# A front written in another order, and weight conversions, batch 0's tail and local scores at other steps, in an attention and mixer kernel

## The chip, the core and the metric

The kernel runs on one core of a Trainium2 chip. The metric is the device time of one execution in microseconds. The core has a matrix engine (PE, with PEld for its weight loads), a vector engine (DVE), a scalar engine (ACT), a third elementwise engine (POOL), and queues that start transfers (SP, and ACT's own). Each engine works through its own instructions in order; an instruction that waits holds all that stand behind it on that engine.

## What is computed

Attention of 8 batches with 8 heads over 576 positions of 64 numbers, and behind it a mixer block on the 576 x 512 result of each batch:

```python
scores = scale * np.matmul(q, k.transpose(0, 1, 3, 2))
rel = pos[:, None] - pos[None, :]
mask_local = (rel >= 0) & (rel < stride)                       # heads 0 to 3, stride 32
mask_strided = (rel >= 0) & (pos[None, :] % stride == pos[:, None] % stride)   # heads 4 to 7
attn = softmax(np.where(masks, scores, -1e9))                  # softmax stands for the written-out lines
x = (attn @ v).transpose(0, 2, 1, 3).reshape(B, S, H * D)
xt = x.transpose(0, 2, 1)
h = np.maximum(xt @ w_tok1, 0.0) @ w_tok2                      # token mix, 576 -> 256 -> 576
u = x + h.transpose(0, 2, 1)
out = u + np.maximum(u @ w_ch1, 0.0) @ w_ch2                   # channel mix, 512 -> 1536 -> 512
```

The mixer's weights come as 64-bit floats, everything else as 32-bit ones.

## The kernel before, in words

**Products.** A wide matrix product is made of three passes in a reduced float format: each operand is split into a high part and a low part, and high x high, high x low and low x high are added (names end in `h` and `l`, as `w1h`, `w1l`).

**Weights.** They must be converted from 64 bits and split first. `convert` does it for a piece of at most 128 x 512 in three stages: the load (L118); on ACT the low byte (L128) and the high word (L131), on DVE the sign byte (L129); then the putting together on DVE (L133), the cast to the high part on ACT (L142) and the subtraction that leaves the low part on POOL (L143). `pieces` lists the 22 pieces that are still to be converted when the channel mix of batch 0 begins: nine of `w1`, twelve of `w2`, and the tail of the second token weight. `do_pieces(i)` runs stage two of piece i+1, stage three of piece i, and the loads of pieces three or four further on.

**The front** (to about 44 us) loads batch 0's operands, computes its attention (`s0`, `s1` strided heads, `l0`, `l1` local heads), converts the token weights and the first three pieces of `w1` (`e0` to `e7`), does the token mix (`L` for the local half, `S` for the strided half, `m0` to `m3`), and begins the pieces (`p0` to `p3`). Each of these is a generator, and the text `order` says which one takes its next step; `b` is a product without use that keeps PE busy, and `x` reloads the strided half of the attention's result from DRAM. All engines' queues and SP's are filled in this order.

**The channel mix.** `mlp` runs 24 blocks for each batch: `up_proj(fc)` (12 products, `w1`, L825) and `down_proj(fc)` (12 products, `w2`, L837), as up 0, up 1, up 2, down 0, up 3, down 1, and so on. Behind an up block ACT makes `gh` (L828) and DVE `gl` (L829); the single bank of `up_proj` (`h`) is free for the next up block when both are done. After block n the work that stands under step n in `after` is put into the queues, in its middle that of step n - 0.5. Step n has nothing to do with time: it is a place in each engine's order. In batch 0 this work is:

- the conversions, `do_pieces(i)`, by a formula in i;
- batch 0's tail, `tok2_tail` (L632 on PE, L633 on ACT, L634 on DVE, and a store of SP, L635), the last 64 positions;
- batch 1's strided heads (`lanes`): scores (L391, L394, L400, L401, L404), transposition (L410, copies L412), values (L421, L428 to L432, stores L442);
- batch 1's remaining local heads (`rest`, four units): load, scores (L197, then L216 on DVE and L219 on ACT), transposition (L224, copy L226), values (L232, L237 to L247, store L258);
- from step 12 the load of batch 1's rows (L546, L549), from 15 its token mix (`tok1`: splits L561 on ACT, L564 and L567 on DVE, products L579 on PE, then L587 and L588; `tok2`: L613, L618 at steps 20 and 22);
- from step 14 the later batches' strided heads on POOL and DVE (products L453, sums L506 and L533; loads L467 in ACT's queue).

Score, transposition and value products take their banks (`t`) from three in turn. From the channel mix on, SP's order is made by a scheduler from the program; that of PE, DVE, ACT and POOL is the written one.

## Time and profile before

| | us |
|---|---|
| median of three runs (795.97 to 799.19) | 797.36 |
| the profiled execution | 799.21 |
| its span in the trace | 797.4 |
| PE busy | 770.7 |
| DVE, ACT, POOL busy | 463.4, 241.4, 379.4 |

The span is the time from the first to the last instruction in the trace; what lies around it is 1.8 us. A busy PE isn't PE at its peak: its clock has two levels, and the granted clock of a stretch is given as a share of the higher one. A timeline row shows when an instruction (or a run of like ones) began, how long it took, and in brackets how long its engine stood idle before it and what ended that.

### The profile page before, as it was taken

The page shows a single profiled execution, that of the slowest core. Times are in us where ns is not written, and L with a number is a line of the kernel's source. Part 1 is how long each engine was busy: PE and PEld are TensorE (multiplying, and loading weights), DVE is VectorE, ACT ScalarE, POOL GpSimd, SP SyncE. Part 2 cuts the span into 40 slices and gives each one's busy share as a digit, 9 for nine tenths or more (in the row PEclk, how much of TensorE's full clock was granted, in tenths as well). Part 3 has the DMA queues.
Part 4 walks back from the last instruction along what each step waited for, and adds up shares of the span by engine and source line. Part 5 has one row for each costly group of instructions (what it writes and reads, how often), then busy time and mean ns, then how long its engine had stood idle before and what let it go on. Part 6 is the DMA issues. An engine that isn't in the chain of part 4 may idle for free.

```text
span 797.4 us, 14592 instructions
## 1 busy us (share of the span) xinstructions
PE 770.7 (97%) x5916; PEld 623.6 (78%) x5916; DVE 463.4 (58%) x963; ACT 241.4 (30%) x496; POOL 379.4 (48%) x287
## 2 busy tenths in 40 slices
PE   7889997999999999999999999999999999999998
PEld 4767776877778888887888888788888888888886
DVE  4756658778588776876687758776652233113112
ACT  4776864132112322331223122332232222102010
POOL 2232357958877883778478766667500000202000
PEclk9999999999999999999999999999999999999999
DMA  9776682235802471356215521645043211101001
GB/s 323 239 253 212 189 256 81 94 108 152 247 22 97 117 232 43 111 148 241 83 67 162 146 83 54 191 157 152 0 127 105 55 47 72 53 1 53 1 1 53
DMA packets 72731, 96.20 MB, mean 121 GB/s; under 512 B 33560, under 2 KB 47704, under 8 KB 72664
## 3 DMA queue, kind: packets, MB, share of 16 engines
q1 hardware_dynamic: 72088, 93.38, 37.7%
q10 hardware_dynamic: 576, 1.90, 0.6%
q8 instruction: 46, 0.75, 0.4%
q14 instruction: 21, 0.17, 0.1%
HBM read 67.79 MB, written 27.46 MB: 119 GB/s over the span
## 4 chain that ended last, share of the span: by engine, by line
PE 76%; DVE 9%; DMA 5%; POOL 4%; issue 2%; ACT 2%; SPq 1%; DVEq 0%; ACTq 0%; POOLq 0%
PE acc L837 31%; PE h L825 28%; PE t L618 5%; PE t L579 5%; POOL sprod L453 4%; PE t L825 2%; DMA w_raw<-in_wt 2%; DMA sa<-in_qs 1%; PE t L357 1%; DVE sa L533 1%; DVE xhl L567 1%; PE t L632 1%; DVE w_f L133 1%; DVE w_rest L129 1%; DVE ss L506 1%
## 5 line engine op out<-in xcount | busy, mean ns | idle before, releaser
L453 POOL TENSOR_TENSOR sprod<-sa,ss 128x576 f32<-128x576 f32 (+8 forms) x108 | 153.5, 1460 | 84.9 <-issue 49.0
L453 POOL TENSOR_TENSOR sprod<-sa 128x576 f32<-128x576 f32 (+8 forms) x108 | 160.8, 1520 | 38.4 <-DVE ss L506 13.5
L837 PE MATMUL acc<-gh,w2h 128*128 128x512 f32 x432 | 170.8, 395 | 0.0
L829 DVE SCALAR_TENSOR_TENSOR gl<-h,gh 128x512 fp32r<-128x512 f32 x99 | 68.1, 688 | 176.3 <-ACT gh L828 176.0
L837 PE MATMUL acc<-gl,w2h 128*128 128x512 f32 x432 | 168.5, 390 | 0.0
L837 PE MATMUL acc<-gh,w2l 128*128 128x512 f32 x432 | 168.4, 390 | 0.0
L825 PE MATMUL h<-uh,w1h 128*128 128x512 f32 x396 | 157.8, 399 | 2.5 <-DVE gl L829 2.4
L825 PE MATMUL h<-ul,w1h 128*128 128x512 f32 x396 | 155.0, 391 | 0.0
L825 PE MATMUL h<-uh,w1l 128*128 128x512 f32 x396 | 154.6, 390 | 0.0
L828 ACT ACTIVATE gh<-h 128x512 fp32r<-128x512 f32 x99 | 59.1, 597 | 289.0 <-PE h L825 289.0
L837 PEld LDWEIGHTS acc<-gh,w2h 128*128 128x128 f32 x432 | 81.3, 188 | 17.3
L837 PEld LDWEIGHTS acc<-gh,w2l 128*128 128x128 f32 x432 | 81.2, 188 | 17.2
L506 DVE TENSOR_REDUCE ss<-sprod 128x9 f32<-128x576 f32 (+8 forms) x108 | 80.2, 777 | 24.5 <-POOL sprod L453 24.4
L837 PEld LDWEIGHTS acc<-gl,w2h 128*128 128x128 f32 x432 | 81.3, 188 | 16.5 <-DVE gl L829 0.2
L825 PEld LDWEIGHTS h<-uh,w1h 128*128 128x128 f32 x396 | 74.5, 188 | 20.7 <-DVE gl L829 4.6
L533 DVE TENSOR_REDUCE sa<-sprod 128x64 f32<-128x576 f32 (+8 forms) x108 | 80.1, 777 | 17.2 <-POOL sprod L453 16.9
L825 PEld LDWEIGHTS h<-ul,w1h 128*128 128x128 f32 x396 | 74.5, 188 | 16.0
L825 PEld LDWEIGHTS h<-uh,w1l 128*128 128x128 f32 x396 | 74.5, 188 | 14.6
L646 POOL TENSOR_TENSOR x<-x,xhl 128x512 f32<-128x512 f32 x4 | 5.0, 1284 | 115.1 <-DMA x<-u 115.1
L579 PE MATMUL t<-xhl,t1h 128*128 128x512 f32 (+1 forms) x134 | 41.2, 390 | 5.1 <-DVE xhl L564 2.5
L561 ACT CAST xhl<-x 128x512 fp32r<-128x512 f32 (+1 forms) x37 | 21.9, 609 | 42.7 <-PE t L579 36.4
L567 DVE TENSOR_TENSOR xhl<-x,xhl 128x512 fp32r<-128x512 f32 (+1 forms) x30 | 29.3, 996 | 9.2 <-ACT xhl L561 9.2
(190 smaller groups left out, 872.3 us busy)
## 6 DMA issues: line engine op xcount, KB each, us to landing
out_t<-ot SPq DMA_DIRECT2D x35, 256.0 KB
w_raw<-in_w SPq DMA_DIRECT2D x17, 512.0 KB
lqk<-in_qkU SPq DMA_DIRECT2D x9, 832.0 KB
x<-x SPq DMA_DIRECT2D x28, 256.0 KB
lv<-in_vU SPq DMA_DIRECT2D x9, 780.0 KB
xhl<-in_w SPq DMA_DIRECT2D x7, 512.0 KB
x<-lv SPq DMA_DIRECT2D x36, 96.0 KB
xtl<-lv SPq DMA_DIRECT2D x36, 96.0 KB
```

The source lines that it names most:

```text
L129: nc.vector.tensor_scalar(out=y_b[:, :, 3], in0=raw_b[:, :n, 7], scalar1=128, scalar2=None, op0=ALU.bitwise_and)
L453: i = nc.gpsimd.tensor_tensor(op=op, **operands)
L506: nc.vector.tensor_reduce(out=s_t[:, i, :i + 1], in_=pr.rearrange("p (n d) -> p n d", d=D), axis=AX.X, op=ALU.add)
L533: nc.vector.tensor_reduce(out=o_t[:, i], in_=pr.rearrange("p (d n) -> p d n", n=i + 1), axis=AX.X, op=ALU.add)
L561: nc.scalar.copy(out=xh, in_=x)
L567: apart.append(nc.vector.tensor_tensor(out=xlo, in0=x, in1=xh.bitcast(F32), op=ALU.subtract))
L579: nc.tensor.matmul(ph[m], l[:, c, P * m:P * m + P], r, start=(c == 0 and k == 0), stop=(c == NSC - 1 and k == len(terms) - 1))
L618: nc.tensor.matmul(pu, l[:, cs], r[:, m, :MAIN], start=(turned and m == 0 and k == 0), stop=(m == 1 and k == 2), skip_group_check=True)
L825: nc.tensor.matmul(ph, l[:, cc, fs], r, start=(cc == 0 and k == 0), stop=(cc == NCC - 1 and k == 2))
L828: nc.scalar.activation(out=gh, in_=ph, func=AF.Relu)
L829: nc.vector.scalar_tensor_tensor(out=gl, in0=ph, scalar=0.0, in1=gh.bitcast(F32), op0=ALU.max, op1=ALU.subtract)
L837: nc.tensor.matmul(acc[cc], l[:, fc, cs], r, start=(fc == 0 and k == 0), stop=(fc == NFC - 1 and k == 2))
```

## The change

Three tables are changed; no instruction of the computation is added or taken away but twelve more rows of keep-busy products and their weight loads on PE.

- `order`, the front, is written anew. The strided pair `s1` goes first, the operands of both local pairs are loaded ahead of the first token weight, the second token weight's conversion goes behind both local softmaxes, and the reload `x` and the later weights' loads move as well.
- `do_pieces(i)` stood at int(1.8 i)/2, so 0, 0.5, 1.5, 2.5, ... up to 18.5; it stands at int(1.6 + 1.48 i)/2, so 0.5, 1.5, 2, 3, 3.5, ... up to 16. The staging memory is given back at step 18, before at 20.
- Batch 0's tail moves from step 2 to 3. The scores of the four local units move from steps 1.5, 4.5, 7.5, 9.5 to 2.5, 5.5, 8.5, 10, their transpositions and values with them (the last one's values stay at 11.5), and the loads of units two to four from 2, 5, 7 to 3, 6, 9.

```diff
--- before.py
+++ after.py
@@ -769,9 +769,9 @@
                 nc.gpsimd.tensor_copy(out=masks[:, 64 * c:64 * c + 64], in_=mask_sb[:, FIRST.get(c, 0)])
 
         order = """
-            s0 s1 s1 l0 s0 s0 s1 e0 s0 l0 e0 l0 s0 l1 e1 s1 b e2 l0 e0 e1 l1 l1 b s1 e3 e2 e4 l1 b b e1 s0 s1 e2 e3 e5
-            l0 l1 e4 b b b b m0 L x L L L e3 L e4 L l0 m1 S m3 m0 e6 m0 S e5 S S S e7 e6 S m2 e5 m1 m2 e6 p0 m3 m1 l1 m2 m3 e7 e7
-            p1 p2 p3 p0"""
+            s1 s0 s1 s1 s0 s0 l0 s1 b l0 l0 b s1 b l1 e0 e1 s0 l0 e0 l1 l1 b e0 s0 b b b e2 e3 e1 e2 s1 s0
+            l1 e4 e1 e2 l0 b l1 b b b b b x e3 e5 m0 L e4 L L L e6 e3 e4 L m1 L m3 e7 S m0 l0 S m0
+            e5 S S p0 S e6 e5 m2 S m1 e7 e6 m2 m1 l1 m2 m3 m3 p0 e7 p1 p2 p3"""
 
         for i, k in enumerate(order.split()):
             if i == 3:
@@ -982,7 +982,7 @@
         def do_tail(cc):
             x_next["u"].append(tail_u(up0, ps_t, x_next["x"], cc))
 
-        at(2 if b == 0 else 0, tok2_tail, ps_t, x_t, h, b)
+        at(3 if b == 0 else 0, tok2_tail, ps_t, x_t, h, b)
         if b + 1 < B:
             at(12, load_next, b + 1)
             steps = (15, 16, 17, 18, 19, 19) if b < 2 else range(14, 20)
@@ -999,15 +999,15 @@
                 at(20 + cc, do_tail, cc)
         if b == 0:
             for i in range(len(pieces)):
-                at(int(1.8 * i) / 2, do_pieces, i)
+                at(int(1.6 + 1.48 * i) / 2, do_pieces, i)
             for i in (0, 1, 2, 3, 4, 6, 7, 8):
                 at(i, next, lanes[0], None)
-            for g, steps in zip(rest, ((0, 1.5, 2.5, 3.5), (2, 4.5, 5.5, 6.5), (5, 7.5, 8.5, 9.5), (7, 9.5, 10.5, 11.5)), strict=True):
+            for g, steps in zip(rest, ((0, 2.5, 3.5, 4.5), (3, 5.5, 6.5, 7.5), (6, 8.5, 9.5, 10.5), (9, 10, 11, 11.5)), strict=True):
                 for i in steps:
                     at(i, next, g, None)
             at(12, first_ends)
             at(14, first_strided)
-            at(int(0.9 * len(pieces)) + 1, staging_ends)
+            at(18, staging_ends)
         for k, steps in UNITS[b].items():
             for n, i in enumerate(steps):
                 if i is not None:
```

The first place is DVE's order at the front, from the first strided softmax on: L129 takes the sign bytes of a weight (`w_raw`), L283 and L284 are a local softmax, L428 to L432 divide a strided result. Before:

```order
L129 TENSOR_SCALAR w_rest0_101<-w_raw_223 128x512
L283 TENSOR_REDUCE lm_282<-pair_238 128x10
L284 TENSOR_TENSOR ls_281<-pair_238,lm_282 128x2x5x64
L428 TENSOR_SCALAR em_190<-pair_286 128x12
L430 RECIPROCAL em_190<-em_190 128x12
L432 TENSOR_TENSOR ex_311<-pair_286,em_190 128x3x128 x2
L133 SCALAR_TENSOR_TENSOR w_f_234<-w_f_234,w_rest0_101 128x512
L129 TENSOR_SCALAR w_rest1_102<-w_raw_319 128x512
L283 TENSOR_REDUCE lm_392<-pair_348 128x10
L284 TENSOR_TENSOR ls_391<-pair_348,lm_392 128x2x5x64
```

and after:

```order
L283 TENSOR_REDUCE lm_277<-pair_233 128x10
L284 TENSOR_TENSOR ls_276<-pair_233,lm_277 128x2x5x64
L428 TENSOR_SCALAR em_185<-pair_282 128x12
L430 RECIPROCAL em_185<-em_185 128x12
L432 TENSOR_TENSOR ex_307<-pair_282,em_185 128x3x128 x2
L129 TENSOR_SCALAR w_rest0_101<-w_raw_316 128x512
L283 TENSOR_REDUCE lm_384<-pair_340 128x10
L284 TENSOR_TENSOR ls_383<-pair_340,lm_384 128x2x5x64
L133 SCALAR_TENSOR_TENSOR w_f_335<-w_f_335,w_rest0_101 128x512
```

The first local softmax has no weight ahead of it any more, and the second one the first weight instead of the second.

The second place is PE's order in the channel mix of batch 0, from the middle of block 2 (`up_proj(2)`) on; L197 are the scores of the first local unit, L632 the tail, L410 the strided transposition. Before:

```order
L197 MATMUL t<-lqk 32x64 x16
L825 MATMUL h<-uh,w1h 128x512
L825 MATMUL h<-uh,w1l 128x512
L825 MATMUL h<-ul,w1h 128x512
L825 MATMUL h<-uh,w1h 128x512
L825 MATMUL h<-uh,w1l 128x512
L825 MATMUL h<-ul,w1h 128x512
L632 MATMUL t<-hh_142,t2h 128x512
L632 MATMUL t<-hl_143,t2h 128x512
L632 MATMUL t<-hh_144,t2h 128x512
L632 MATMUL t<-hl_145,t2h 128x512
L410 MATMUL t<-ident,es 128x128 x6
```

and after, where block 2 has ended and block 3 (`down_proj(0)`, L837) comes:

```order
L410 MATMUL t<-ident,es 128x128 x6
L837 MATMUL acc_816<-gh,w2h 128x512
L837 MATMUL acc_816<-gl,w2h 128x512
L837 MATMUL acc_816<-gh,w2l 128x512
L837 MATMUL acc_817<-gh,w2h 128x512
L837 MATMUL acc_817<-gl,w2h 128x512
L837 MATMUL acc_817<-gh,w2l 128x512
L197 MATMUL t<-lqk 32x64 x16
L837 MATMUL acc_818<-gh,w2h 128x512
```

The scores moved from the middle of block 2 into the middle of block 3, the tail behind that block, and the strided transposition is now the first thing behind block 2.

The third place is ACT's order from `gh` of block 14 on; L128, L131 and L142 are conversions, L467 the loads of the strided heads, L561 the splits of batch 1's rows. Before, `w_raw_1528`, `w_raw_1615` are the pieces 17 and 18:

```order
L828 ACTIVATE gh_1623<-h_1601 128x512
L128 ACTIVATE w_rest1_102<-w_raw_1528,small_69 128x512
L131 ACTIVATE w_f_1627<-w_raw_1528 128x512
L142 CAST w1h_72<-w_f_1608 128x4x128
L467 DMA sa_1637<-in_ks 128x1152
L467 DMA sa_1636<-in_qs 128x1152
L467 DMA sa_1638<-in_vs 128x1152
L561 CAST xhl_1659<-x_1565 128x512
L128 ACTIVATE w_rest0_101<-w_raw_1615,small_69 128x512
L131 ACTIVATE w_f_1662<-w_raw_1615 128x512
L142 CAST w2h_794<-w_f_1627 128x512
```

and after, where `w_raw_1614`, `w_raw_1631`, `w_raw_1657` are the pieces 19, 20 and 21:

```order
L828 ACTIVATE gh_1646<-h_1633 128x512
L128 ACTIVATE w_rest1_102<-w_raw_1614,small_69 128x512
L131 ACTIVATE w_f_1650<-w_raw_1614 128x512
L142 CAST w1h_72<-w_f_1624 128x4x128
L467 DMA sa_1660<-in_ks 128x1152
L467 DMA sa_1659<-in_qs 128x1152
L467 DMA sa_1661<-in_vs 128x1152
L128 ACTIVATE w_rest0_101<-w_raw_1631,small_69 128x512
L131 ACTIVATE w_f_1674<-w_raw_1631 128x512
L142 CAST w2h_799<-w_f_1650 128x512
L561 CAST xhl_1689<-x_1586 128x512
L128 ACTIVATE w_rest1_102<-w_raw_1657,small_69 128x512
```

Before the first split one piece is begun and one cast is done, now two of each. In SP's order the load of piece 17 stood between batch 1's last rows; now pieces 17 and 18 stand ahead of the last local store (L258) and pieces 19 to 21 behind all of the rows.

## Rows read from the trace of the kernel before

**Rows 1.** the page: span, and share of the engines

```profile
span 797.4 us, 14592 instructions
...
PE 770.7 (97%) x5916; PEld 623.6 (78%) x5916; DVE 463.4 (58%) x963; ACT 241.4 (30%) x496; POOL 379.4 (48%) x287
```

**Rows 2.** busy time by stretch: engine busy us (x instructions), granted clock, DMA share, GB/s

```profile
49.80:69.90 20.10, 17.68 (x208) 13.00 (x208) 11.34 (x36) 12.35 (x26) 5.06 (x6) 0.83 0.67 212
69.90:101.20 31.30, 30.04 (x396) 22.84 (x395) 20.67 (x71) 24.58 (x49) 13.56 (x11) 1.00 0.68 204
101.20:112.10 10.90, 10.90 (x49) 8.82 (x47) 4.40 (x8) 6.55 (x11) 4.86 (x4) 1.00 0.79 220
112.10:137.20 25.10, 19.16 (x85) 14.86 (x85) 19.40 (x21) 13.71 (x24) 17.75 (x13) 1.00 0.43 148
...
56.20:62.90 6.70, 5.95 (x17) 4.33 (x16) 2.90 (x14) 5.23 (x13) 0.46 (x1) 0.50 0.60 200
138.00:141.40 3.40, 3.40 (x10) 2.63 (x9) 1.96 (x3) 0.59 (x1) 3.40 (x3) 0.50 0.60 180
```

**Rows 3.** timeline of DVE at the front: start us, us, instruction [idle before <-releaser]

```profile
13.43 0.47 DVE L129 TENSOR_SCALAR w_rest<-w_raw 128x512 uint8<-128x512 uint8 x1 [3.12 <-DMA w_raw<-in_wt]
...
19.22 0.80 DVE L129 TENSOR_SCALAR w_rest<-w_raw 128x512 uint8<-128x512 uint8 x1 [1.76 <-DMA w_raw<-in_wt]
19.91 0.80 DVE L283 TENSOR_REDUCE lm<-pair 128x10 f32<-128x640 f32 x1
```

**Rows 4.** timeline of PE at the front

```profile
29.15 0.50 PE L579 MATMUL t<-eqk,t1h 128*128 128x256 f32 x2 [0.90 <-ACT eqk L561]
...
44.30 0.39 PE L825 MATMUL h<-uh,w1h 128*128 128x512 f32 x1
```

**Rows 5.** timeline of PE, steps 1.5 to 2 of batch 0

```profile
54.15 0.30 PE L197 MATMUL t<-lqk 64*32 64x64 f32 x2 [0.87 <-DVE gl L829]
55.24 0.45 PE L197 MATMUL t<-lqk 64*32 64x64 f32 x30 [0.80 <-DVE es L401]
...
58.91 0.80 PE L632 MATMUL t<-hh,t2h 128*128 128x512 f32 x1 [0.75 <-POOL t2h L143]
```

**Rows 6.** timeline of ACT: one conversion, and the copies behind a transposition

```profile
83.05 0.85 ACT L412 COPY es<-t 128x384 f32<-128x384 f32 x2
...
86.39 0.87 ACT L128 ACTIVATE w_rest<-w_raw,small 128x512 uint8<-128x512 uint8 x1
87.12 0.66 ACT L131 ACTIVATE w_f<-w_raw 128x512 f32<-128x512 f32 x1
88.19 0.62 ACT L142 CAST w2h<-w_f 128x512 fp32r<-128x512 f32 x1 [0.41 <-DVE w_f L133]
```

**Rows 7.** timeline of PE, step 9.5

```profile
92.99 0.45 PE L197 MATMUL t<-lqk 64*32 64x64 f32 x30 [1.26 <-DVE lx L247]
```

**Rows 8.** timelines of SP and ACT around step 14

```profile
100.86 0.36 SPq L258 DMA_DIRECT2D x<-lx  x1
...
104.58 0.36 SPq L118 DMA_DIRECT2D w_raw<-in_w  x1
...
110.46 0.90 ACT L128 ACTIVATE w_rest<-w_raw,small 128x512 uint8<-128x512 uint8 x1 [3.01 <-DMA w_raw<-in_w]
```

**Rows 9.** timeline of PE, steps 16 to 20

```profile
113.66 0.74 PE L579 MATMUL t<-xhl,t1h 128*128 128x512 f32 x2 [1.40 <-ACT xhl L561]
...
128.99 0.73 PE L579 MATMUL t<-xhl,t1h 128*128 128x512 f32 x2 [1.08 <-DVE xhl L564]
...
136.81 0.44 PE L613 MATMUL t<-ident,x 128*128 128x128 f32 x2 [3.45 <-DVE hl L588]
```

**Rows 10.** timelines of POOL and DVE, steps 18 to 20

```profile
122.78 1.57 POOL L453 TENSOR_TENSOR sprod<-sa 128x576 f32<-128x576 f32 x1
...
122.99 1.68 DVE L129 TENSOR_SCALAR w_rest<-w_raw 128x512 uint8<-128x512 uint8 x1
...
130.31 2.03 DVE L133 SCALAR_TENSOR_TENSOR w_f<-w_f,w_rest 128x512 uint32<-128x512 uint32 x1
```

## The prediction

> **What bounds the kernel now.** I read the page first: PE is busy 770.7 of 797.4 us [rows 1]; DVE, ACT and POOL are far below. So only stretches in which PE waits, or runs at half clock, can give time back, and the change touches only what comes before about 140 us (the front, and batch 0's 24 blocks). Second, the table by stretch [rows 2]. Blocks 0 and 1 of batch 0 end at 49.8; block 4 (`up_proj(3)`) at 69.9, block 12 at 101.2, block 16 at 112.1, and the next batch's token mix reaches its second half at 137.2. The first of these stretches runs at a mean clock of 0.83, with 56.2 to 62.9 at 0.50, the 1.2 GHz level; 138.0 to 141.4 is at 0.50 as well. From 112.1 to 137.2 PE is busy 19.16 of 25.1 us. Third, the timelines of PE name the waits. At the front the first mixing product starts at 29.15 and block 0 at 44.30 [rows 4]. In block 2 and behind it PE waits 0.87, 0.80 and 0.75 us [rows 5], and then the clock falls. At step 9.5 it waits 1.26 for a bank [rows 7]. At steps 16 to 20 it waits 1.40, 1.08 and 3.45 [rows 9], the last two for DVE, whose conversions run at 1.5 to 2.0 us each there [rows 10].
>
> **The change, part by part.** All sums are against the profiled execution (799.21 us: a span of 797.4 and 1.8 around it); the median of the runs is 797.36, 1.85 less, and I carry the difference over to it.
>
> *Front order: -3.0 us.* Before, DVE's queue holds the second local softmax (L283) behind the high bytes of the second token weight, which land at 19.2 [rows 3]. After, only the first token weight stands ahead of it, and it is loaded behind the local operands. It is then the tenth load of the queue with 4.73 MB up to its end; before, 3.38 MB landed at 13.4 and 5.25 MB at 19.2 [rows 3], so it lands at about 17.6 and L283 starts some 1.9 us earlier than its 19.91. The two local value products no longer stand back to back on PE, so DVE divides the first while PE makes the second: about 0.9 more, which brings the first mixing product [rows 4] to about 26.3. Four transpositions move ahead of the last mixing products, 0.2. Downstream the conversions of the token and first up weights keep their place relative to PE, so nothing takes this back before block 0. Bounds: -1.2 (the weight lands as late as 19.2 and only the overlap counts) to -3.5. The added keep-busy products lie in gaps.
>
> *Local scores at 2.5 and batch 0's tail at 3: -4.9 us.* Both leave the place where their banks and the tail weight are not ready. Gone are the three waits, 2.4 us [rows 5], and the half clock that follows them: 6.7 us with PE busy 5.95 [rows 2] is 3.0 us lost. New: the first down block now follows block 2 directly, and its third product needs the low part of `w2` chunk 0, which POOL makes after ACT's cast; I put that at 0.7 us, and a bank for the local scores at 0.3. -5.4 + 1.0 is -4.4; laid out by durations, the stretch of 20.1 us shrinks to 14.8, -5.3; I take the middle. Bounds: -1 (the waits reform at the new place and the clock falls again) to -5.5.
>
> *Conversions at 0.74 step apiece: +3.5 us in steps 4 to 12.* One conversion is 1.8 us of ACT (starts 86.39, 87.12, 88.19 less a wait of 0.41, and 0.53 for the cast) [rows 6], plus that wait where the multiply-out on DVE is late. Before, ACT is busy 12.35 + 24.58 + 6.55 = 43.5 of the 62.3 us to 112.1 [rows 2]. After, four more conversions fall into the same steps: 7.2 us, and 21 waits of 0.41 are 8.6, together 59 of 62. ACT, off the path so far, becomes nearly full, and it does two conversions, 3.6 us, where before there was one between an exponential and the copies that free its banks. That is where I expect new PE waits: step 7 (transpositions behind a late exponential) 0.6, step 7.5 (local value products, whose bank is freed by L412, half of 0.85 [rows 6]) 2.2, step 8.5 a bank behind DVE 0.85, step 10 the last local operands, whose load now stands in SP's queue behind six strided stores and a weight, 0.8; and 0.3 elsewhere. The 1.26 of step 9.5 [rows 7] goes. Sum 4.75 - 1.26 = +3.5. Bounds: 0 (ACT keeps up) to +8 (each up block also waits for its `gh`).
>
> *Steps 12 to 16:* PE ran without a gap, 10.9 of 10.9 [rows 2], and should again: nothing.
>
> *Steps 14 to 20: -2.3 us.* Before, ACT stands 3.01 us at 110.46 for a weight that SP issued at 104.58, in the midst of the next batch's rows, which wait for the store of 100.86 [rows 8]: 5.9 us from issue to use. After, one weight more goes ahead of that store, and the next (the third last) goes behind the rows. I expect the same wait on ACT, from the same store, and behind it not one conversion but two before the first split of the next batch (L561): 1.8 + 0.4 more. So the 1.40 becomes about 3.65: +2.25. Behind it, though, no conversion is left for steps 18 to 20: the last cast comes at step 16 instead of 18.5, ahead of most of POOL's strided products. DVE's splits and `hl` are then on time, and 1.08 + 3.45 [rows 9] go. Sum -2.3. Bounds: -4.5 to +3 (the wait grows and the 3.45 stays).
>
> *Clock: 0.* The half clock of 138.0 to 141.4 cost 3.4 / 2 = 1.7 us [rows 2] and came behind 3.45 us of waiting. It goes with it, but a wait of 3.65 at step 16 should bring one of the same price. Bounds: -1.7 to +2.
>
> Later batches keep their order on every engine; the shift passes to the end one to one. Sum: -3.0 - 4.9 + 3.5 - 2.3 + 0 = **-6.7**: 792.5 for a profiled execution, **790.7** as a median.
>
> **A rule against the change.** Rows: DVE's L129 starts at 122.99 inside a POOL product that runs 122.78 to 124.35, and takes 1.68 us; L133 took 2.03 at 130.31 [rows 10], against 0.47 for L129 at 13.43 [rows 3]. So where POOL is at work, a conversion's steps on DVE can be held. The Trainium skill ("SBUF — State Buffer", SBUF: two separate sides) says that DVE in a two-port mode or with two SBUF inputs and GpSimd lock a shared port pair against each other for a whole instruction; by that rule denser conversions, each with a POOL subtraction, would hold each other, and the trace agrees at the rows named.
>
> **The rivals.**
>
> 1. *ACT keeps up.* The waits of steps 7 to 10 don't form (+3.5 becomes 0): 787.2. For it: ACT had idle time next to its waits; against it: 59 of 62 us. Chance 0.15.
>
> 2. *The end of batch 0 keeps its waits.* `hl` (L588) still stands on DVE behind three sums of POOL's strided products; if the first of these start late, the 3.45 and the 1.08 remain: -6.7 + 4.5, 795.2. For it: POOL's strided work begins only after all conversions; against it: its loads are issued in the same step. Chance 0.28.
>
> 3. *Slower: DVE and POOL hold each other.* Each of the 17 conversions of steps 3 to 16 takes 1.0 us more (1.5 to 2.0 in place of 0.5 to 0.7) and ACT waits for it: 59 + 17 = 76 us where there were 62.3, +13.5 in place of -4.9 + 3.5; with -3.0 and -2.3 that is about +8: 805. It decides from about ten of the 17 (3 us of slack, then the 6.7). Against it: in 44 to 112 us few of DVE's conversion steps are stretched, since POOL starts only after ACT's cast, when DVE is past its own. Chance 0.10.
>
> 4. *The new numbers move less than they say* (an engine's order stays as it was): the order shown above excludes it for DVE, PE and ACT. Chance 0.02.
>
> **How the numbers follow.** The forecast, 790.7, has 0.45. Its own bounds (front -1.2 to -3.5, tail -1 to -5.5, conversions 0 to +8, end -4.5 to +3, clock -1.7 to +2) seldom fall together: about 785 to 797. To hold 8 in 10 the range takes in rivals 1 and 2 and leaves out rival 3: **785.0 to 798.5**. Half a per cent, 4.0 us, is about what a measurement of this kernel tells from no change, so faster means below 793.4: most of the forecast (0.39), rival 1 (0.15) and a little of rival 2: 0.57. Within: 0.32. Slower, above 801.3: rival 3 and a remainder, 0.11.
>
> **What would show each step right or wrong.** Front: the first mixing product near 26.3 and block 0 near 41.3; wrong, if DVE's L283 of the second pair still starts after 19. Steps 1 to 4: a clock of 1.00 there and about 15 us from the end of block 1 to the end of block 4. Steps 4 to 12: a wait of about 2 us for L412 at the value products of step 7.5, and a stretch of about 35 us for 31.3. Step 16: a wait of 3 to 4 us for ACT's L561, half clock behind it. Step 20: no wait for L588. The forecast is wrong most easily by ACT's queue, which I laid out by hand, and by where the clock falls.

## The result and the profile after

The changed kernel takes 805.05 us (median of seven runs, 800.92 to 805.69) against 797.36: a ratio of 1.0084, 95% interval 1.0057 to 1.0111. It is slower by 0.8%, where 790.7 was forecast; the time lies above the whole range. Run again beside 23 runs of the kernel before (e5 below) it took 802.10, ratio 1.0055 (1.0035 to 1.0075). The profiled execution is 805.69 us with a span of 803.9, 6.5 more than before. Three executions of the runs below that lie far off the rest (two at a granted clock of 0.75 throughout, 951 us, one of them the profiled one of e9, and one of the kernel before at 3870 us) are left out of the ratios. The page after, against [rows 1]:

```profile
span 803.9 us, 14601 instructions
PE 775.7 (96%) x5915; PEld 627.1 (78%) x5921; DVE 462.6 (58%) x963; ACT 241.6 (30%) x496; POOL 378.8 (47%) x287
```

PE is 5 us busier for the same products of the computation (the new front adds five keep-busy products, each under 0.7 us), so clock is lost as well as time. The table by stretch, with the columns of [rows 2] (us, busy time of PE, PEld, DVE, ACT, POOL, granted clock, DMA share, GB/s): blocks 2 to 4, blocks 5 to 12, blocks 13 to 16, and from there to the second half of the next batch's token mix; behind the dots three pieces of these at about half clock:

```profile
50.94:65.70 14.76, 14.12 (x175) 10.88 (x175) 8.51 (x27) 10.08 (x22) 4.04 (x4) 1.00 0.66 194
65.70:107.60 41.90, 35.18 (x428) 25.12 (x427) 25.83 (x81) 28.93 (x58) 16.45 (x14) 0.92 0.64 197
107.60:119.00 11.40, 11.16 (x48) 8.56 (x46) 4.25 (x6) 5.04 (x8) 4.74 (x4) 1.00 0.65 195
119.00:144.90 25.90, 20.42 (x83) 16.73 (x84) 15.40 (x21) 11.89 (x20) 18.29 (x14) 0.87 0.46 164
...
84.50:88.00 3.50, 3.45 (x48) 2.31 (x52) 0.89 (x5) 0.62 (x2) 0.97 (x1) 0.59 0.78 213
98.30:103.00 4.70, 4.62 (x73) 3.29 (x74) 1.53 (x13) 2.95 (x8) 2.53 (x2) 0.64 0.53 177
122.00:130.00 8.00, 5.52 (x14) 4.38 (x15) 4.26 (x5) 5.93 (x10) 5.13 (x4) 0.57 0.69 276
```

Beside [rows 2], between the same places in the program (the windows above meet them within 0.2 us):

| | before | forecast | after | e5, the same again |
|---|---|---|---|---|
| block 0 starts | 44.3 | 41.3 | 45.2 | 45.1 |
| blocks 2 to 4 | 20.2 | 14.8 to 15.2 | 14.8 | 14.9 |
| blocks 5 to 12 | 31.3 | 34.8 | **41.9** | **39.3** |
| blocks 13 to 16 | 10.9 | 10.9 | 11.4 | 11.3 |
| block 16 to the tail products of batch 1 (L632) | 44.1 | 41.8 | 43.5 | 41.3 |
| L632 to the end | 641.3 | 641.3 | 641.6 | 641.8 |

Blocks 2 to 4 came out as laid out, the front gained nothing, and blocks 5 to 12 took three times the extra that was forecast. The waits that do it, in the timeline of PE, against [rows 5, 7, 9]:

```profile
57.54 0.50 PE L837 MATMUL acc<-gh,w2l 128*128 128x512 f32 x1 [0.64 <-POOL w2l L143]
...
67.97 0.56 PE L232 MATMUL t<-lv,ls 64*32 64x65 f32 x32 [0.72 <-ACT ls L226]
...
80.33 0.88 PE L410 MATMUL t<-ident,es 128*128 128x128 f32 x6 [1.58 <-ACT es L404]
...
84.55 0.46 PE L232 MATMUL t<-lv,ls 64*32 64x65 f32 x30 [1.72 <-ACT es L412]
...
91.16 0.45 PE L197 MATMUL t<-lqk 64*32 64x64 f32 x30 [0.37 <-DVE ex L432]
...
98.38 0.62 PE L197 MATMUL t<-lqk 64*32 64x64 f32 x32 [2.07 <-DMA lqk<-in_qkT]
...
124.48 1.22 PE L579 MATMUL t<-xhl,t1h 128*128 128x512 f32 x2 [5.50 <-ACT xhl L561]
```

The waits of [rows 5] and the 1.08 and 3.45 of [rows 9] are gone, the 1.40 is 5.50, and blocks 5 to 12 hold five waits of 0.37 us or more where they held one.

**How the wait of step 7 comes about.** ACT, in front of the exponential of the strided scores (L404), and DVE beside it:

```profile
73.55 0.88 ACT L128 ACTIVATE w_rest<-w_raw,small 128x512 uint8<-128x512 uint8 x1
...
75.34 1.09 ACT L219 ACTIVATE ls<-ls,lm 128x64 f32<-128x64 f32 x4
76.31 0.61 ACT L828 ACTIVATE gh<-h 128x512 fp32r<-128x512 f32 x1
79.53 0.75 ACT L404 ACTIVATE es<-es 128x648 f32<-128x648 f32 x1 [2.62 <-DVE es L401]
```

```profile
76.95 0.69 DVE L829 SCALAR_TENSOR_TENSOR gl<-h,gh 128x512 fp32r<-128x512 f32 x1 [2.31 <-ACT gh L828]
77.56 0.48 DVE L400 TENSOR_REDUCE em<-t 128x6 f32<-128x324 f32 x1
```

The scores were done at 75.6. DVE could have begun their maximum (L400) then, but in its order `gl` (L829) stands first, which needs `gh`, and on ACT `gh` stands behind a conversion (73.55 to 75.34) and the local exponentials (L219). So L400 starts at 77.56, L404 at 79.53, and PE waits 1.58. Behind it two more conversions stand ahead of the copies (L412) that free the banks for L232: 1.72.

**The waits of steps 10 and 16** start in SP's queue:

```profile
91.50 2.26 SPq L442 DMA_DIRECT2D x<-ex  x6
93.87 0.36 SPq L118 DMA_DIRECT2D w_raw<-in_w  x1
94.33 0.56 SPq L186 DMA_DIRECT2D lqk<-in_qkT  x1
...
112.37 0.81 SPq L546 DMA_DIRECT2D x<-x  x2
...
114.47 6.70 SPq L118 DMA_DIRECT2D w_raw<-in_w  x3
```

```profile
119.45 0.87 ACT L128 ACTIVATE w_rest<-w_raw,small 128x512 uint8<-128x512 uint8 x1 [4.25 <-DMA w_raw<-in_w]
...
123.80 0.62 ACT L561 CAST xhl<-x 128x512 fp32r<-128x512 f32 x1
```

The one operand buffer of the local units is free at 91.6, when the third unit's scores are done; its next load stands behind six strided stores and a weight, starts at 94.33 and is used at 98.38. Of the last three pieces the first two stand on ACT ahead of L561: their loads follow the rows of batch 1, which wait for the last local store, are issued at 114.47 and land at 119.4; L561 comes at 123.80.

### The profile page after: what moved, and what is told of

Its sections match the earlier page's. It is cut to its first block, busy times and chain, and to the rows that moved or that the text cites. A ratio compares the mean times of both kernels' runs of the same rounds, so it can differ in the third digit from the quotient of the medians.

```text
span 803.9 us, 14601 instructions
## 1 busy us (share of the span) xinstructions
PE 775.7 (96%) x5915; PEld 627.1 (78%) x5921; DVE 462.6 (58%) x963; ACT 241.6 (30%) x496; POOL 378.8 (47%) x287
## 4 chain that ended last, share of the span: by engine, by line
PE 74%; DVE 9%; DMA 5%; POOL 4%; ACT 3%; issue 2%; SPq 2%; ACTq 0%; DVEq 0%; POOLq 0%
PE acc L837 30%; PE h L825 26%; PE t L579 5%; PE t L618 4%; POOL sprod L453 4%; PE t L825 2%; DMA w_raw<-in_w 1%; DVE sa L533 1%; DVE gl L829 1%; DMA sa<-in_vs 1%; PE t L357 1%; PE t L632 1%; DVE xhl L567 1%; DVE w_rest L129 1%; ACT w_rest L128 1%
## 5 line engine op out<-in xcount | busy, mean ns | idle before, releaser
L453 POOL TENSOR_TENSOR sprod<-sa 128x576 f32<-128x576 f32 (+8 forms) x108 | 160.2, 1517 | 41.2 <-DVE ss L506 15.5
L837 PE MATMUL acc<-gh,w2h 128*128 128x512 f32 x432 | 171.7, 397 | 0.0
L837 PE MATMUL acc<-gh,w2l 128*128 128x512 f32 x432 | 169.4, 392 | 0.6 <-POOL w2l L143 0.6
L837 PE MATMUL acc<-gl,w2h 128*128 128x512 f32 x432 | 169.2, 392 | 0.0
L829 DVE SCALAR_TENSOR_TENSOR gl<-h,gh 128x512 fp32r<-128x512 f32 x99 | 68.0, 687 | 174.8 <-ACT gh L828 174.5
L837 PEld LDWEIGHTS acc<-gh,w2l 128*128 128x128 f32 x432 | 81.6, 189 | 18.7 <-POOL w2l L143 1.4
L837 PEld LDWEIGHTS acc<-gh,w2h 128*128 128x128 f32 x432 | 81.7, 189 | 17.6
L837 PEld LDWEIGHTS acc<-gl,w2h 128*128 128x128 f32 x432 | 81.7, 189 | 16.6 <-DVE gl L829 0.2
L825 PEld LDWEIGHTS h<-uh,w1l 128*128 128x128 f32 x396 | 74.6, 188 | 14.6
L579 PE MATMUL t<-xhl,t1h 128*128 128x512 f32 (+1 forms) x134 | 41.8, 396 | 8.0 <-ACT xhl L561 5.5
L579 PEld LDWEIGHTS t<-xhl,t1h 128*128 128x128 f32 x134 | 24.8, 192 | 15.2 <-ACT xhl L561 6.4
```

What stands on the lines that cost most here:

```text
L453: i = nc.gpsimd.tensor_tensor(op=op, **operands)
L579: nc.tensor.matmul(ph[m], l[:, c, P * m:P * m + P], r, start=(c == 0 and k == 0), stop=(c == NSC - 1 and k == len(terms) - 1))
L825: nc.tensor.matmul(ph, l[:, cc, fs], r, start=(cc == 0 and k == 0), stop=(cc == NCC - 1 and k == 2))
L829: nc.vector.scalar_tensor_tensor(out=gl, in0=ph, scalar=0.0, in1=gh.bitcast(F32), op0=ALU.max, op1=ALU.subtract)
L837: nc.tensor.matmul(acc[cc], l[:, fc, cs], r, start=(fc == 0 and k == 0), stop=(fc == NFC - 1 and k == 2))
```

## The experiments

Ratios are to the kernel before, whose runs were interleaved. Stretches are read between the same places as in the table above. Each expectation names a theory and a rival; behind each result stands which of the two it met.

### One part alone: e1, e2, e3

e1: the new front on the kernel before.

```diff
-            s0 s1 s1 l0 s0 s0 s1 e0 s0 l0 e0 l0 s0 l1 e1 s1 b e2 l0 e0 e1 l1 l1 b s1 e3 e2 e4 l1 b b e1 s0 s1 e2 e3 e5
+            s1 s0 s1 s1 s0 s0 l0 s1 b l0 l0 b s1 b l1 e0 e1 s0 l0 e0 l1 l1 b e0 s0 b b b e2 e3 e1 e2 s1 s0
...
```

> The kernel before with the new front alone. What was predicted: block 0 starts 3 us earlier, a time of about 794.4 (ratio 0.996). In the trace of the changed kernel block 0 starts at 45.20 instead of 44.30, and PE makes the first strided scores in 1.29 us a group instead of 0.77 from 5.27 us on, though no instruction ahead of them has changed. Theory: the order itself gains 3 us and the half speed at the start takes 4 us back in some executions; then either block 0 starts at about 41 (time 794) or it starts at about 45 with 1.29 us a group (time 798), and no middle. Rival: the order gains nothing even at full speed (0.77 a group), since the wait of 2.29 at the second strided values and DVE's order set the end; then block 0 starts at 43.5 or later with 0.77 a group, ratio 1.000 or more.

Measured: 796.14, ratio 0.9981 (0.9962 to 0.9999). PE, with the first scores at full speed:

```profile
5.38 0.77 PE L394 MATMUL pair<-eqk 64*54 64x54 f32 x22 [0.77 <-DMA eqk<-in_qksT]
...
20.67 0.82 PE L421 MATMUL pair<-ev,es 64*64 64x65 f32 x31 [2.45 <-issue]
...
28.46 0.51 PE L579 MATMUL t<-eqk,t1h 128*128 128x256 f32 x2 [0.43 <-ACT eqk L561]
```

and DVE's second local softmax:

```profile
17.50 0.82 DVE L283 TENSOR_REDUCE lm<-pair 128x10 f32<-128x640 f32 x1 [0.20 <-PE pair L276]
```

L283 comes at 17.50, earlier than the 18.0 of the forecast. But PE stands 2.45 us in the middle of the second strided values, for nothing that the profile shows, and goes on at 20.67; before it went on at 20.70 after such a wait of 1.48. What DVE wins is spent there, and behind it, where the clock is at 0.50 from 21.1 to 24.5 (before, from 22.0 to 25.4). Block 0 starts at 43.97, 0.3 earlier: the rival in the trace, though the ratio is under its 1.000. In this trace blocks 2 to 4, in their old order, took 16.7 us, with the tail's wait of 1.61 but no half clock.

e2: tail and local scores alone.

```diff
-        at(2 if b == 0 else 0, tok2_tail, ps_t, x_t, h, b)
+        at(3 if b == 0 else 0, tok2_tail, ps_t, x_t, h, b)
...
-            for g, steps in zip(rest, ((0, 1.5, 2.5, 3.5), (2, 4.5, 5.5, 6.5), (5, 7.5, 8.5, 9.5), (7, 9.5, 10.5, 11.5)), strict=True):
+            for g, steps in zip(rest, ((0, 2.5, 3.5, 4.5), (3, 5.5, 6.5, 7.5), (6, 8.5, 9.5, 10.5), (9, 10, 11, 11.5)), strict=True):
```

> The kernel before with batch 0's tail at step 3 and the local scores at steps 2.5, 5.5, 8.5, 10 (and their followers), front and conversions as before. Predicted term: -4.9 us, and the trace of the changed kernel gives 14.8 us for the 20.1 between the ends of blocks 1 and 4, so -5.3. Theory: this part is a gain of its own and the later waits come from the conversions: ratio 0.994 (792.5), stretch from the end of block 4 to the end of block 12 near 31 us. Rival: the later scores are what makes the waits at steps 7 to 10 (their load and their banks collide whatever the conversions do): 5 us or more are given back there, ratio 1.000 or above, that stretch 36 us or more.

Measured: 798.87, ratio 1.0004 (0.9989 to 1.0019). Blocks 5 to 12:

```profile
65.20:99.30 34.10, 31.60 (x427) 23.20 (x427) 21.15 (x75) 25.00 (x51) 14.00 (x11) 1.00 0.63 197
```

34.1 us: waits of 0.69, 0.78 and 1.02 (the load at step 10), and PE busy 1.56 us more than in [rows 2]: 32 products (x427, before x396) have moved into this stretch from the one before. Blocks 2 to 4 took 16.3, at full clock: alone, the moved scores make a wait of 2.25 there, for the exponential (L404) ahead of the strided transposition. Between theory and rival; the time is the rival's.

e3: conversions (and the tail, which must come behind its weight).

```diff
-                at(int(1.8 * i) / 2, do_pieces, i)
+                at(int(1.6 + 1.48 * i) / 2, do_pieces, i)
...
-            at(int(0.9 * len(pieces)) + 1, staging_ends)
+            at(18, staging_ends)
```

> The kernel before with the conversions at 0.74 step apiece (staging memory back at 18) and the tail at step 3, which the conversions' places need; local scores and front as before. Theory: the denser conversions alone cost what the changed kernel loses (10.6 us from the end of block 4 to the end of block 12, of it 5 us half clock), and the wait for L561 at step 16 is over 4 us; of the half clock at block 2 the tail's move saves 1 to 3: ratio 1.008 (804). Rival: the loss needs the later scores as well (their waits are for banks freed late by ACT); alone the conversions cost under 2 us there and the wait at step 16 is all that is new: ratio 0.999 (797).

Measured: 796.81, ratio 0.9982 (0.9968 to 0.9995). Blocks 5 to 12:

```profile
66.70:100.90 34.20, 30.85 (x395) 23.12 (x395) 22.26 (x72) 27.35 (x55) 15.19 (x12) 1.00 0.69 212
```

34.2 us, with five waits of 0.2 to 0.95; 2.62 at step 16, none at steps 18 to 20, so the stretch from block 16 to L632 is 39.9 for 44.1. The rival in the main (it had under 2 us in blocks 5 to 12): alone the conversions lose 2.9 there and 0.9 in blocks 13 to 16, and win 4.

### Both, and one taken out: e4, e5, e6

e4: the changed kernel with the conversions of before (the diff of e3 reversed, the tail left at 3).

> The changed kernel with the conversions at 0.9 step apiece and the staging memory given back at 20, as before; front, tail and local scores as changed. Theory: this takes out all of the loss between blocks 4 and 12 and the wait of 5.50 at step 16, and leaves the gain of 5.3 at blocks 2 to 4, with the front at -3 or +0.9: 789.5 to 793.5, ratio 0.990 to 0.995. Rival: the waits at steps 7 to 10 stay because of the later scores: 798 or more, ratio 1.000 or above.

Measured: 797.29, ratio 0.9991 (0.9976 to 1.0007). Blocks 2 to 4 took 14.6, blocks 5 to 12 34.1 as in e2, and the 1.08 and 3.42 at steps 18 to 20 are there again. Between theory and rival: the later scores cost their 2.8 without the denser conversions.

e5: the changed kernel once more.

> The changed kernel once more, to see which of its losses come in every execution. Its trace has half clock behind the waits of steps 7.5, 10 and 16 (PE busy 5.1 us longer for the same blocks from block 4 to 12) and half speed at the first strided scores. Theory: the waits (about 1.6 at L410, 1.7 at L232, 2.1 at L197, 5.5 at L579) stand in the order and come again within 0.5 us each, the fall of the clock behind each does not have to; 801 to 806, ratio 1.008. Rival: the waits themselves are chance (a transfer that landed late); then this trace has less than half of the 10.9 us.

Measured: 802.10, ratio 1.0055. Blocks 5 to 12, and waits:

```profile
65.80:105.10 39.30, 32.04 (x427) 23.09 (x427) 25.75 (x81) 28.96 (x58) 16.33 (x14) 1.00 0.68 209
```

```profile
97.40 0.58 PE L197 MATMUL t<-lqk 64*32 64x64 f32 x32 [2.21 <-DMA lqk<-in_qkT]
...
120.19 0.73 PE L579 MATMUL t<-xhl,t1h 128*128 128x512 f32 x2 [3.82 <-ACT xhl L561]
```

The theory for blocks 5 to 12: the waits come again within 0.4 us (L410 1.56 and L232 1.74), while no half clock comes behind them. The wait at step 16 is 3.82 for 5.50, more apart than the theory allowed, with half clock behind it. So each of the two edits costs 2.8 to 2.9 us in blocks 5 to 12, and both together 8.0 at full clock, up to 10.6 with half clock.

e6: the changed kernel with units two to four back.

```diff
-((0, 2.5, 3.5, 4.5), (3, 5.5, 6.5, 7.5), (6, 8.5, 9.5, 10.5), (9, 10, 11, 11.5))
+((0, 2.5, 3.5, 4.5), (3, 4.5, 5.5, 6.5), (5, 7.5, 8.5, 9.5), (8, 9.5, 10.5, 11.5))
```

> The changed kernel with the second, third and fourth local unit's scores, transpositions and values at steps 4.5, 7.5, 9.5 (and followers) as before; the first unit, the tail, the conversions and the front as changed. Theory: the loss needs both, dense conversions and these units a step later; with the units back the stretch from the end of block 4 to the end of block 12 is 34 us instead of 41.9, no half clock in it, the wait at step 16 is 2.6 as with the conversions alone, and the 5.3 us of blocks 2 to 4 stay: 791 to 794, ratio 0.991 to 0.995. Rival: the loss comes from the conversions with the shifted start of the channel mix (front and first unit), so that stretch stays over 38 us: 800 or more.

Measured: 798.98, ratio 1.0013 (0.9993 to 1.0032). The edit made a wait of its own, 2.31 for a bank: the second unit's scores now stand behind the first unit's values in the same step. With half clock behind it and again at 96 to 100, blocks 5 to 12 took 39.6. The waits of 1.56 and 1.74 at steps 7 and 7.5 are gone, though, with the conversions as dense as in the changed kernel; in e4, with the later units, they are 0.74 and none. So these two waits need both edits. The time is better than the changed kernel's; on the size of the sum it decides nothing.

### The order within a step: e9, e13, e14, e17

e9, e13: the changed kernel with the loop of the conversions written behind those of the attention, and one piece moved.

```diff
-            for i in range(len(pieces)):
-                at(int(1.6 + 1.48 * i) / 2, do_pieces, i)
...
+            for i in range(len(pieces)):
+                at(6 if i == 7 else int(1.6 + 1.48 * i) / 2, do_pieces, i)
             at(12, first_ends)
```

> The changed kernel with the conversion of a step put into the queues behind that step's attention work (scores, exponentials, copies) instead of ahead of it, and the piece of step 5.5 at step 6, so that it doesn't stand ahead of gh of block 6; steps otherwise as changed. Theory: the waits of 1.56 for L404 at step 7 and 1.74 for L412 at step 7.5 come from the order on ACT and DVE, two conversions ahead of an exponential and of the copies; both fall under 0.5, and the stretch of blocks 5 to 12 from 39.3 to about 36.5: 799.5, ratio 1.001. Rival: ACT is simply full in these steps (58 of 62 us with its own waits), so whatever stands behind is late: the waits pass to gh (up blocks wait for L829) or to the low parts of the weights, and the time is 801 or more.

Measured: 798.39, ratio 1.0001 (0.9986 to 1.0017): better than the theory. The same kernel once more, for its trace:

> The same kernel as in the run with the attention work ahead of the conversions (798.4, ratio 1.000), for a trace at the usual clock. Theory (order on ACT and DVE): the waits for L404 at step 7 and L412 at step 7.5, 1.56 and 1.74 us, are under 0.5 each, the one for the load of the fourth unit at step 10 is under 1, and the stretch from the end of block 4 to the end of block 12 is 35 to 36.5 us instead of 39.3. Rival: the waits are still there and the gain was made elsewhere (at step 16, or in the front); then that stretch is over 38.

Measured: 797.63, ratio 0.9993 (0.9976 to 1.0010). Blocks 5 to 12 and blocks 13 to 16, and waits:

```profile
63.10:98.90 35.80, 32.10 (x427) 23.55 (x428) 23.39 (x77) 28.04 (x57) 16.40 (x13) 1.00 0.71 214
98.90:113.20 14.30, 11.51 (x49) 8.51 (x47) 8.95 (x14) 9.43 (x15) 7.38 (x6) 1.00 0.67 220
```

```profile
80.21 0.46 PE L232 MATMUL t<-lv,ls 64*32 64x65 f32 x30 [1.40 <-ACT es L412]
...
90.83 0.58 PE L197 MATMUL t<-lqk 64*32 64x64 f32 x32 [1.05 <-DMA lqk<-in_qkT]
...
103.29 0.50 PE L825 MATMUL h<-uh,w1h 128*128 128x512 f32 x1 [1.64 <-DVE gl L829]
```

The theory, in the main: the wait for L404 is gone and 3.5 us of blocks 5 to 12 come back; the load of step 10 now starts right behind the stores. But L412 keeps 1.40, and in blocks 13 to 16 up blocks wait 1.64 and 1.15 for `gl`: 3 us lost there, the rival's share of e9. Four and a half us of the median are won. (This trace also starts block 0 at 42.6, 2.5 earlier than e5, by nothing that the edit touches.)

e14: the same edit on e3 (units at their old steps).

> The kernel before with the conversions at 0.74 step, the tail at step 3 and the conversions behind the attention work of their step (local units and front as before). Theory: the conversions' cost of 2.9 us in blocks 5 to 12 is the order on ACT and DVE too (0.75 for L432, 0.51 for L401, 0.91 for L412), so about 1.5 goes: 795.3, ratio 0.9965. Rival: with the units at their old places the order within a step no longer matters, 796.8 as without the edit, ratio 0.998.

Measured: 799.71, ratio 1.0019 (1.0002 to 1.0036), 2.9 worse than e3. Nothing is won in blocks 5 to 12 (35.3) and the waits for `gl` (1.65, 1.17) and one of 0.94 for a cast come. Worse than the rival: with the units at their old steps the edit doesn't help.

e17: e13 with four conversions moved from ahead of a `gh`.

```diff
-                at(6 if i == 7 else int(1.6 + 1.48 * i) / 2, do_pieces, i)
+                at({7: 6, 15: 12, 17: 14, 20: 16}.get(i, int(1.6 + 1.48 * i) / 2), do_pieces, i)
```

> The changed kernel with the conversions behind the attention work of their step and four of them moved so that none stands between the middle of an up block and its gh on ACT, or comes in pairs ahead of one (piece 7 from 5.5 to 6, 15 from 11.5 to 12, 17 from 13 to 14, 20 from 15.5 to 16). Theory: the waits of 1.64 and 1.15 for gl at blocks 14 and 16 go and blocks 13 to 16 take 11.3 us again; the wait for L561 at step 16 falls from 1.9 to about 1, since one conversion less stands ahead of it: 793.5 to 795 (ratio 0.995), faster than both kernels. Rival: the late loads hold ACT wherever the conversions stand, and what is not waited at gh is waited at L561 (3 us or more): 797 or more, ratio 0.999.

Measured: 800.00, ratio 1.0016 (1.0000 to 1.0031). The waits for `gl` go (blocks 13 to 16 take 10.9), and PE's wait at step 16, with ACT ahead of it, is:

```profile
118.74 1.22 PE L579 MATMUL t<-xhl,t1h 128*128 128x512 f32 x2 [6.94 <-ACT xhl L561]
```

```profile
111.35 0.88 ACT L128 ACTIVATE w_rest<-w_raw,small 128x512 uint8<-128x512 uint8 x1 [4.22 <-DMA w_raw<-in_w]
```

The rival: a piece whose load stands behind the rows holds ACT for 4.22 us here, for 4.25 in the changed kernel.

### The waits of steps 10 and 16: e10, e7, e8, e11, e12, e18

e10: the fourth unit's scores at 10.5 in place of 10.

> The changed kernel with the fourth local unit's scores at step 10.5 instead of 10. Theory: the 2.2 us at step 10 is the load of its operands, which can start only when the third unit's scores (step 8.5) have freed the one buffer and stands in SP's queue behind six strided stores; half a step more is 1.4 us, so the wait falls to 0.8 or less, and nothing else moves: 1.4 us less, 800.5 (ratio 1.0035). Rival: transposition and values then follow in half a step each, and wait for the exponential and the copy: the 1.4 comes back at step 11 as 1.5 or more, ratio 1.0055 or above.

Measured: 801.09, ratio 1.0037 (1.0021 to 1.0053). In place of the 2.2 there is 0.32 for the load, 0.90 for a bank that the third unit's values (now in the same step) free, and 0.57 behind. Between theory and rival in the trace; the ratio is the theory's, but its interval overlaps that of e5, so the 1 us of the median is not shown to be won.

e7: the first split of the rows a step earlier.

```diff
-            steps = (15, 16, 17, 18, 19, 19) if b < 2 else range(14, 20)
+            steps = (14 if b == 0 else 15, 16, 17, 18, 19, 19) if b < 2 else range(14, 20)
```

> The changed kernel with the first split of batch 1's rows (L561) put into ACT's queue at step 14 instead of 15, so ahead of the conversions of the pieces 19 and 20. Theory: the 5.50 us at step 16 is the queue of ACT: these pieces' loads were issued at 114.47, behind the rows', and landed at 119.4, and L561 stood behind both conversions, while the rows had landed by 118. With L561 ahead, PE waits under 1 us at step 16 and the half clock of 122 to 131 does not come: 6 to 8 us less, 797 to 799 (ratio 1.000). Rival: the rows themselves come late (issued at 112.37 behind a store, used at 118 or later), or the w2 pieces are late for blocks 17 and 19; then the wait moves and less than 3 us are won, 802 or more.

Measured: 803.73, ratio 1.0076 (1.0055 to 1.0098). The first products no longer wait; the second ones do, for a split that still stands behind the conversions:

```profile
127.24 1.22 PE L579 MATMUL t<-xhl,t1h 128*128 128x512 f32 x2 [5.30 <-ACT xhl L561]
```

The rival. e8 joins e6 and e7, e11 joins e7, e9 and e10, e12 is e7's edit on e3, e18 on e17:

> The changed kernel with the second to fourth local units back and the first split at step 14, both edits of the two runs before it. Theory: both gains add: 5.3 us less than before in blocks 2 to 4, 3 more in blocks 5 to 12, no wait at step 16 and none at steps 18 to 20 (4.5 less, and the half clock of 138 to 141): 788 to 791, ratio 0.988 to 0.991. Rival: with the units back the wait at step 16 is already small, so the early split gives nothing: the same time as without it, within 0.3%.

Measured: 797.57, ratio 0.9997 (0.9976 to 1.0018). With the units back the early split does help in the trace (1.11 is left, at the second split, and block 16 to L632 takes 37.3), but e6's own wait stays: neither.

> The changed kernel with three edits: conversions behind the attention work of a step (one piece from 5.5 to 6), fourth unit's scores at 10.5, first split of batch 1's rows at step 14. Theory: the waits of steps 7, 7.5 and 10 go (4 us), the one at step 16 shrinks from 3.8 to about 1 since the last pieces are no longer late, and no half clock follows: 794 to 795, ratio 0.996. Rival: one full engine (ACT) keeps the sum of waits: 799 or more.

Measured: 801.12, ratio 1.0038 (1.0017 to 1.0059). A wait of 3.18 for a bank at step 10.5, and half clock: the rival.

> The kernel before with the conversions at 0.74 step, the tail at step 3 and the first split of batch 1's rows at step 14; front and all local units as before. Theory: without the later units the conversions cost 2.9 us in blocks 5 to 12 and give 4 back at steps 16 to 20, and the early split takes the wait of 2.62 at step 16 away (with units near their old places it took 2.6): 794 (ratio 0.995), the fastest of all. Rival: the early split only moves that wait to the second split, as it did in the changed kernel: 796.8 as without it (ratio 0.998).

Measured: 796.50, ratio 0.9982 (0.9965 to 0.9999). The wait of 2.62 becomes 1.25 and 0.70 at the second and third split: no different from e3.

> The same with the first split of batch 1's rows at step 14. Theory: the wait at step 16 goes below 0.5 us and nothing takes its place: 793 to 794, ratio 0.994. Rival: the split now stands ahead of a conversion and the rows land only by then, so ACT and with it gh of block 14 wait for the rows: no gain, or up to 2 us more than without it.

Measured: 799.01, ratio 1.0013 (0.9995 to 1.0030). The first wait moves to the second split (3.64).

### The front: e15, e16

e15: e1 with two loads behind the first strided stores.

```diff
-... b e0 s0 b b b e2 e3 e1 e2 s1 s0
+... b e0 s0 b b b e1 s1 e2 e3 s0 e2
```

> The kernel before with the new front, and in it the loads of the last piece of the first token weight and the first of the second (0.75 MB) issued behind the first strided stores, at about 18 us instead of 9 to 11; all other engines' orders as in the new front. Theory: the wait of 2.45 us in the second strided values (L421) ends when the loads ahead of it have passed, so it ends about 1.9 us earlier, at 18.6 to 19, the first mixing product starts at 26.6 to 27.4 instead of 28.46, and the time is 795 (ratio 0.996). Rival: the end of the wait at 20.4 to 20.7 doesn't depend on the loads; then L421 goes on at the same time, and the later weights cost something behind it: ratio 0.998 or above.

Measured: 796.82, ratio 0.9981 (0.9963 to 0.9998). Inconclusive: here the first scores ran at 1.29 a group, so that the second values came only at 21.11 and found no wait. e16 joins this front and e14:

> The two edits before together: conversions at 0.74 step behind the attention work of their step, tail at step 3, local units as before, new front with the two loads later. Theory: both gains add, 793.5 to 795, ratio 0.9945 to 0.9965, and faster than both kernels. Rival: the gains of the channel mix are eaten by half clock that comes by chance behind waits of 0.5 to 1 us; then 796 to 797, ratio 0.998, as each part alone.

Measured: 799.41, ratio 1.0006 (0.9990 to 1.0021), as e14; the wait, 1.90, ends at 19.84, earlier than in e1 (20.67), but as early as without the late loads in e13 (19.86). So neither run shows that the loads set it.

## Why the prediction was wrong, point by point

Between the profiled execution that was forecast (792.5 us) and the one measured (805.69) lie 13.2 us: 7.1 in blocks 5 to 12, 3.9 in the front, 1.8 from block 16 to L632, 0.4 in all the rest.

**Front, -3.0 (bounds -1.2 to -3.5): measured +0.9.** The step that failed is the one from DVE to PE: that freeing the second softmax on DVE's queue brings the first mixing product forward to 26.3. With the first scores at full speed the softmax came early (17.50 in e1), but PE's own wait in the second strided values, 1.48 in the trace of before and not priced, took most of the gain: the first mixing product came at 28.46. A second step failed behind it, that nothing takes the gain back before block 0: from the first mixing product to block 0 the same 96 products take 15.1 to 15.2 us in the five traces with the old front, and 15.5 to 16.5 in the 14 with the new one (e9 left out); why is open. Two more losses came with the new order, seen at its start:

```profile
5.27 1.29 PE L394 MATMUL pair<-eqk 64*54 64x54 f32 x22 [0.22 <-DMA eqk<-in_qksT]
...
11.31 1.54 PE L410 MATMUL pair<-ident,es 128*128 128x128 f32 x6
...
45.20 0.50 PE L825 MATMUL h<-uh,w1h 128*128 128x512 f32 x1
```

In 12 of those 14 traces the first scores wait 0.2 to 1.9 us for their operands, with the old front in 1 of 5; and in this one they and all up to 13.5 run at half speed, so that even the second softmax came only at 19.28 (19.91 before). Why these operands, whose loads are issued at the same time, land later is open. Where neither happened (e13, e18), block 0 started at 42.6 and 42.5, inside the bounds. In e13:

```profile
19.86 0.69 PE L421 MATMUL pair<-ev,es 64*64 64x65 f32 x31 [2.18 <-issue]
...
26.83 0.50 PE L579 MATMUL t<-eqk,t1h 128*128 128x256 f32 x2 [0.51 <-ACT eqk L561]
```

But the 44.30 of before, from which the bounds count, holds a half clock behind PE's wait (0.50, with PE busy 2.98 of 3.41 us) that the prediction didn't read:

```profile
21.97:25.38 3.41, 2.98 (x69) 2.08 (x72) 2.51 (x6) 2.69 (x7) 0.27 (x1) 0.50 0.48 145
```

In the three traces with the old front that don't have it there (e2, e3, e14), block 0 started at 43.3 to 43.6. Against these, the new front at its best is some 0.8 us ahead, less than the lower bound.

**Tail and first local scores, -4.9: measured -5.4 for this trace, but some 2 for the kernel.** The mechanism was right to the tenth (14.8, clock 1.00, 0.64 for the low part of `w2`). The size was read off one trace: of its 20.2 us, 3 are a half clock that e1 and e15, with the same order and a single wait of 1.6 in place of the three, don't show (16.7 each). And a value product set of 32 products, 0.56 us, that left this stretch was booked as gain here and not as cost in the next.

**Conversions, +3.5 (0 to +8): measured +8.0 at full clock, +10.6 in the profiled execution.** The waits of e5, forecast in brackets: L410 1.56 (0.6), L232 at 7.5 1.74 (2.2), step 8.5 0.77 (0.85), step 10 2.21 (0.8), others 0.98 (0.3): 7.3 for 4.75, and the 1.26 of [rows 7] is gone as said. So the places were right and two sizes wrong: at step 7 it was not a late exponential by one conversion but a chain over `gh` and `gl`; at step 10 the load is bound by the single buffer as well as by SP. PE is busy 2.0 longer, 0.6 of it the products moved in; the rest was not broken down. The remaining 2.6 of the profiled execution are half clock behind the waits. (One conversion adds up to 1.92 us of ACT from [rows 6], not 1.8, which makes the 59 of 62 us some 60; that is not where the step failed.) The cause, as far as shown: scores alone +2.8 (e2, e4), conversions alone +2.9 (e3), both +8.0 (e5), and of these 3.5 are undone by putting the attention's instructions ahead of the conversions (e13); 3 come back as waits for `gl` in blocks 13 to 16. By its busy time ACT is not full (28.96 of 39.3 us in e5); the order in its queue says where PE waits. How much of the 8.0 is order and how much a loaded ACT, no run separates.

**Blocks 13 to 16, 0:** +0.4 to +0.5.

**Steps 14 to 20, -2.3 (-4.5 to +3), and clock 0:** 1.08 and 3.45 went, a wait at step 16 with half clock behind came, as described: 3.82 in e5 for 3.65 forecast, and 44.1 became 41.3, -2.8. In the profiled execution the wait was 5.50 and the stretch -0.6.

Rival 1 fell, and rival 2's waits went. **Rival 3** named the right time (805) by the wrong way, which is luck. In steps 3 to 16 five of the conversions' steps on DVE were held, each begun inside an instruction of POOL, by some 4 us in all; it was to decide from ten of 17. Two of them (in the first the piece's raw bytes lie in `xhl`), with POOL's:

```profile
70.86 1.57 DVE L129 TENSOR_SCALAR w_rest<-xhl 128x512 uint8<-128x512 uint8 x1
...
93.76 1.77 DVE L133 SCALAR_TENSOR_TENSOR w_f<-w_f,w_rest 128x512 uint32<-128x512 uint32 x1
```

```profile
70.81 1.30 POOL L143 TENSOR_TENSOR w2l<-w_f,w2h 128x512 fp32r<-128x512 f32 x1 [1.95 <-ACT w2h L142]
...
93.65 1.33 POOL L143 TENSOR_TENSOR w2l<-w_f,w2h 128x512 fp32r<-128x512 f32 x1 [1.62 <-ACT w2h L142]
```

The Trainium skill ("SBUF — State Buffer", SBUF: two separate sides) describes such a hold for a whole instruction, where DVE's has two inputs from SBUF, as L133, or is in a two-port mode; the trace agrees at these rows (1.57 for 0.46, 1.77 for 0.67), though it doesn't show in which mode L129, with one input, runs.

What no rival had was the sum: two edits that crowd the same queues in the same steps, each priced nearly alone, and the clock falling behind the waits that they make together.

No version is faster than before by more than 0.2%: e1, e3, e12 and e15 stand at 0.998, with intervals that end just below 1.

## What to carry to other kernels

When two edits put more into the same steps, price the waits with both in the queue: follow one whole chain over the engines (here ACT's `gh`, DVE's `gl`, the softmax, the exponential, the transposition) instead of the next releaser alone. A wait on the critical engine that has no releaser can be a floor under what is freed ahead of it, and a half clock in one trace is no stable loss: see a second execution before booking its removal as a gain.

## What the runs showed of the hardware

The clock's fall behind a short wait is not fixed by the program: in the changed kernel the wait of 1.72 at step 7.5 was followed by a granted clock of 0.59 (84.5 to 88.0), in e5, the same kernel, the one of 1.74 by 1.00; in the front a wait of 2.45 was followed by 0.50 in e1 (21.1 to 24.5) and by 1.00 in e10, with the same front; at step 9.5, a wait of 0.94 in e12 was followed by a granted clock of about 0.66 from 93 to 98, and waits of 0.95 in e3 and e14 by no fall. And the record can miss a fall: from 4.0 to 13.5 in the trace of the changed kernel the granted clock is 1.00 in all rows, while the four groups of first scores took 1.29 us each (0.77 in e1) and the transposition 1.54 (0.87). The Trainium skill ("TensorE: Matmul & The Clock Gate", Seeing it yourself) calls the events of this record unreliable and the durations agree. The wait without a releaser comes in every trace behind the 17th of the 48 second strided products of the new order and behind the 19th of the old one, but for e15. In each of them PE goes on 2.3 to 2.8 us after the start of a 16 KB packet on q8, a queue whose kind the page calls instruction: at 18.07 for 20.67 in e1, at 18.07 for 20.70 before. In e15 that packet starts at 18.45, ahead of the second values (21.11). This points at PE waiting for its own instructions to be loaded; no run changed it, so it is not shown.
